# Transposes of a second row tile set between the first V matmuls, with its layernorm root moved up and a quarter of the first tile normed on ScalarE

## The chip, the cores and the metric

One core of one Trainium2 chip. The time is the device time of one execution in microseconds (us); the span in a profile is from the core's first to its last instruction. Every run named here is of the state fast.

## The reference, cut to what matters

A transformer layer of one sequence: 2048 rows, width 1024, 32 heads of 32, a window of 256, then a feed-forward part of width 3584.

```python
x = A_x
h  = x + attention(layernorm(x) @ wqkv) @ wo       # causal, window 256
h2 = h + silu(layernorm(h) @ w1) @ w2
# layernorm(x) = (x - mean) / sqrt(var + 1e-5), over 1024 columns
```

The first matmul on x comes only after the first 128 rows of x are loaded, normed and transposed (7.93 us after the start in the profile before). That head of the kernel is what the change touches.

## The kernel before: the parts concerned

```python
    load_x(0, 0)                   # row tile 0 of x, 128 x 1024 bf16
    load_wqkv(2 * D)               # V weights, columns 0 to 511: 1 MB
    load_x(0, 1, nc.scalar)
    load_x(0, 2)
    load_wqkv(2 * D + 512)         # V weights, columns 512 to 1023
    load_x(0, 3)
    load_wqkv(0)
    # ... identity; 11 matmuls on zeros: 0.43 us apart up to 5.35 us, then 0.21

    def ln_first(xt, st, rs, j, half_done=None, ahead=None):
        ln_stats(xt, st, j, half_done)              # VectorE: 2 x bn_stats, bn_aggr
        nc.scalar.activation(out=rs[:, j:j + 1], in_=st[:, j, 1:2], func=ACT.Sqrt, bias=eps[:], scale=1.0)
        if ahead is not None:
            ln_half(ahead[0], ahead[1], 0)          # first half of the next tile's statistics
        nc.vector.reciprocal(out=rs[:, j:j + 1], in_=rs[:, j:j + 1])
        for h in range(4):
            ln_norm(xt[:, h * 256:(h + 1) * 256], st, rs, j)     # VectorE

    def turn_first(xt, dst, j):
        for h in range(4):
            for i in range(2):                      # two 128x128 transposes on TensorE into PSUM
                kt = h * 2 + i
                nc.tensor.transpose(out=tp_ps[h][:, i * P:(i + 1) * P], in_=xt[:, kt * P:(kt + 1) * P], identity=ident[:])
            nc.scalar.copy(out=dst[:, h * 2:(h + 1) * 2, j * P:(j + 1) * P],
                           in_=tp_ps[h][:, 0:256].rearrange("p (k q) -> p k q", q=P))

    # v_group(b, j, c, copy, between): 8 matmuls, row tile j times half c of the V weights,
    # then one PSUM copy; between(kt) runs ahead of matmul kt
    ln_first(x_ring[0], st, rs, 0, None, (x_ring[1], half))
    turn_first(x_ring[0], lnT_b[0], 0)
    ln_first(x_ring[1], st, rs, 1, half)

    def turn_1(kt):
        if kt == 7:
            turn_first(x_ring[1], lnT_b[0], 1)

    v_group(0, 0, 0, act, turn_1)
    ln_first(x_ring[2], st, rs, 2)
    v_group(0, 1, 0, act)
    ln_first(x_ring[3], st, rs, 3)
    ln_transpose(x_ring[3], lnT_b[0], 3)            # tile 3 is transposed by a DMA
    # ... three more weight loads
    v_group(0, 0, 1, act)
    turn_first(x_ring[2], lnT_b[0], 2)
    v_group(0, 1, 1, act)
    # ... (0,2,0), (0,2,1), (0,3,0), (0,3,1), then the Q and K groups and all the rest
```

The V groups' matmuls are numbered in their order on TensorE: 1 to 8 is (tile 0, half 0), 9 to 16 (tile 1, half 0), 17 to 24 (tile 0, half 1), the 25th begins (tile 1, half 1).

The softmax here doesn't subtract the row's maximum and nothing guards it: scores larger than these inputs give would overflow.

## Time and profile before

| | before |
|---|---|
| time, median of 3 (later of 6) | 693.14 (693.18) us |
| span of the profiled run | 691.8 us |
| TensorE busy | 99% of the span |
| first x tile landed | 4.42 us |
| first V weight block landed | 7.74 us |
| first transpose, first V matmul, 25th V matmul | 7.04, 7.93, 14.56 us |

The two landings are those of the last part of each transfer on its semaphore. The views that carry the rest are shown in the prediction.

### The profile page before, as it was taken

To read this page: it belongs to the slowest core of one execution; us is meant where nothing else is said; L and a number is where in the kernel's file an instruction comes from. 1 tells how busy PE (TensorE), PEld (TensorE's weight loads), DVE (VectorE), ACT (ScalarE), POOL (GpSimd) and SP (SyncE) were. 2 spreads that over 40 slices of the span, in tenths; PEclk is the share of its full clock that TensorE was granted. 3 is DMA by queue.
4 is the path that set the end of the run, shared out by engine and by line. 5 is a ranking of instruction groups with operands and counts; after the bars stand their busy time and mean duration, and the time that the engine had idled before them with its cause. 6 is when DMAs were issued, how large, how long until landed. Compare 5 with 4: busy or idle time off the path is not lost.

```text
span 691.8 us, 14227 instructions
## 1 busy us (share of the span) xinstructions
PE 686.3 (99%) x6011; PEld 331.3 (48%) x6011; DVE 291.6 (42%) x616; ACT 240.9 (35%) x460; POOL 160.4 (23%) x295
## 2 busy tenths in 40 slices
PE   8999999999999999999999999999999999999998
PEld 3444555555555555544444444444444444444445
DVE  6267646744444439533315133343133251333111
ACT  4316666666766676521310033300133100233000
POOL 1006666656666665500000000000000000000000
PEclk9999999999999999999999999999999999999999
DMA  7732132126241899971023310022300033100010
GB/s 243 259 50 83 36 77 67 26 58 189 72 131 17 240 237 275 213 282 48 14 77 115 91 39 0 1 91 70 84 0 1 9 103 94 39 1 1 30 39 24
DMA packets 76464, 60.96 MB, mean 88 GB/s; under 512 B 50288, under 2 KB 60528, under 8 KB 76400
## 3 DMA queue, kind: packets, MB, share of 16 engines
q1 hardware_dynamic: 76256, 59.78, 31.0%
q8 instruction: 47, 0.77, 0.5%
q10 hardware_dynamic: 144, 0.26, 0.1%
q14 instruction: 17, 0.14, 0.1%
HBM read 39.85 MB, written 8.39 MB: 70 GB/s over the span
## 4 chain that ended last, share of the span: by engine, by line
PE 99%; DMA 1%; DVE 0%; issue 0%
PE hacc L597 19%; PE hacc L634 17%; PE acc L245 17%; PE acc L634 10%; PE acc L597 9%; PE acc L235 8%; PE acc L266 7%; PE o_ps L378 5%; PE sc L298 3%; PE hacc L266 1%; PE sc L350 1%; PE sc L324 1%; DMA r_o<-in_A_x_dram 1%; PE tp L213 0%; DVE ln_st L166 0%; DVE r_o L194 0%
## 5 line engine op out<-in xcount | busy, mean ns | idle before, releaser
L368 POOL TENSOR_SCALAR_AFFINE_SELECT r_e<-r_e 128x512 bf16<-128x512 bf16 (+1 forms) x288 | 157.4, 561 | 127.0 <-ACT r_e L358 63.1
L634 PEld LDWEIGHTS <-r_a 128*128 128x128 bf16 x952 | 90.9, 98 | 103.0
L597 PEld LDWEIGHTS <-r_w 128*128 128x128 bf16 x896 | 87.4, 98 | 105.1
L634 PE MATMUL hacc<-r_a 128*128 128x512 bf16 (+2 forms) x616 | 122.5, 360 | 0.0
L597 PE MATMUL hacc<-r_e,r_w 128*128 128x512 bf16 x456 | 100.9, 379 | 0.0
L310 ACT ACTIVATE r_e<-sc 128x768 bf16<-128x768 f32 x96 | 78.2, 814 | 48.3 <-PE sc L298 46.1
L606 ACT ACTIVATE r_n<-hacc 128x512 f32<-128x512 f32 x30 | 17.9, 597 | 178.9 <-PE hacc L597 178.9
L634 PE MATMUL acc<-r_a 128*128 128x512 bf16 x336 | 74.0, 379 | 0.0
L245 PEld LDWEIGHTS <-r_w 128*128 128x128 bf16 x512 | 44.2, 97 | 46.1 <-issue 1.0
L245 PE MATMUL acc<-r_t,r_w 128*128 128x512 bf16 x256 | 63.4, 379 | 0.0
L247 DVE CAST r_a<-acc 128x512 bf16<-128x512 f32 x56 | 38.6, 690 | 55.8 <-PE acc L245 55.6
L245 PE MATMUL acc<-r_w 128*128 128x512 bf16 x256 | 59.9, 379 | 0.0
L378 PEld LDWEIGHTS <-r_e 128*128 128x128 bf16 x1440 | 47.4, 96 | 17.9
L266 PE MATMUL acc<-r_o,r_a 128*128 128x512 bf16 x208 | 51.9, 379 | 0.0
L597 PE MATMUL acc<-r_e,r_w 128*128 128x512 bf16 x216 | 49.1, 379 | 0.0
L378 PE MATMUL o_ps<-r_a,r_e 128*128 128x33 bf16 x1440 | 48.1, 178 | 0.0
L311 ACT ACTIVATE r_e<-sc 128x256 bf16<-128x256 f32 x96 | 37.6, 392 | 0.0
L649 DVE SCALAR_TENSOR_TENSOR r_t<-hacc,r_t 128x512 bf16<-128x512 f32 (+2 forms) x22 | 14.0, 635 | 55.6 <-PE hacc L634 55.6
L649 DVE SCALAR_TENSOR_TENSOR r_t<-acc,r_t 128x512 bf16<-128x512 f32 x12 | 8.3, 692 | 64.2 <-PE acc L634 64.2
L607 DVE SCALAR_TENSOR_TENSOR r_a<-r_n,hacc 128x512 bf16<-128x512 f32 x30 | 20.6, 688 | 33.0 <-ACT r_n L606 33.0
L597 PE MATMUL hacc<-r_a,r_w 128*128 128x512 bf16 x144 | 32.9, 379 | 0.0
L266 PEld LDWEIGHTS <-r_a 128*128 128x128 bf16 x256 | 21.8, 97 | 22.3
(75 smaller groups left out, 534.2 us busy)
## 6 DMA issues: line engine op xcount, KB each, us to landing
r_w<-in_B_w_dram SPq DMA_DIRECT2D x8, 896.0 KB, 5.1
r_a<-in_B_w_dram SPq DMA_DIRECT2D x7, 1024.0 KB, 7.6
r_w<-in_A_wqkv_dram SPq DMA_DIRECT2D x6, 1024.0 KB, 8.8
h_dram<-r_t SPq DMA_DIRECT2D x16, 256.0 KB, 2.9
r_t<-h_dram SPq DMA_DIRECT2D x16, 256.0 KB, 2.8
out_dram<-r_t SPq DMA_DIRECT2D x31, 128.0 KB, 1.7
r_o<-in_A_x_dram SPq DMA_DIRECT2D x15, 256.0 KB, 3.9
r_e<-h_dram SPq DMA_DIRECT2D x3, 1024.0 KB, 5.6
```

The source lines that it names most:

```text
L235: nc.tensor.matmul(acc, lhsT=lnT_b[b % 2][:, kt, j * P:(j + 1) * P], rhs=wv[:, kt, c * 512:(c + 1) * 512], start=(kt == 0), stop=(kt == KT ...
L245: nc.tensor.matmul(acc, lhsT=wqk[:, kt, col0:col0 + P], rhs=lnT_b[b % 2][:, kt, :], start=(kt == 0), stop=(kt == KT - 1))
L247: copy(out=(qT, kT)[which][b][:, g, :], in_=acc)
L266: nc.tensor.matmul(acc, lhsT=qT[b][:, g, j * P:(j + 1) * P], rhs=wo[:, g, c * 512:(c + 1) * 512], start=(g == 0), stop=(g == G - 1))
L298: nc.tensor.matmul(sc[hh // 2][half * 64:half * 64 + 64, hh % 2, col:col + qb - qa], lhsT=kT[t // 4][r0:r0 + DH, g, k0:k0 + 64], rhs=qT[b] ...
L310: nc.scalar.activation(out=tri[:, :, :, 64:256], in_=both, func=ACT.Exp, scale=scale)
L311: nc.scalar.activation(out=e[:, 1024:1280].rearrange("p (h q) -> p h q", q=P), in_=bank[:, :, 192:320], func=ACT.Exp, scale=scale)
L368: nc.gpsimd.affine_select(out=dst, in_=src, pattern=[[0, n] for n in dst.shape[1:-1]] + [[sgn, P]], compare_op=ALU.is_ge if upper else ALU ...
L378: nc.tensor.matmul(o_ps[pair][:, qt * 2 + hh, 0:VW], lhsT=chunk_of(i, bank, piece, pair, hh), rhs=v[:, b * 4 + kt, g * 4 + pair * 2 + hh, ...
L597: nc.tensor.matmul(acc, lhsT=w1[:, kt, ft * P:(ft + 1) * P], rhs=ln2T[b][:, kt, :], start=(kt == 0), stop=(kt == KT - 1))
L634: nc.tensor.matmul(acc[:, 0:c1 - c0], lhsT=gT[:, ft, j * P:(j + 1) * P], rhs=w2[ft // 4][:, ft % 4, c0:c1], start=(ft == 0), stop=(ft == F ...
L649: nc.vector.scalar_tensor_tensor(out=t_out[j % 2][:, c0:c1], in0=acc[:, 0:c1 - c0], scalar=0.5, in1=t_in[j % 2][:, c0:c1], op0=ALU.mult, o ...
```

## The change

Its intent: take the holes out of TensorE's first seven microseconds. (a) The last quarter of tile 0 is normed on ScalarE as x times 1/sigma plus a shift, so that VectorE reaches tile 1's statistics one instruction sooner. (b) Tile 1's root (the square root of its variance, on ScalarE) goes between tile 0's copies on ScalarE. (c) Tile 1's four pairs of transposes are spread over the end of its predecessor group and the beginning of its own, and the predecessor's PSUM copy is held back behind them. (d) Tiles 2 and 3 are normed in one instruction each.

```diff
 ...
+    def ln_first(xt, st, rs, j, parts, on_act=0):
+        if on_act:
+            shift = small.tile([P, 2], F32, name="ln_shift", tag="ln_shift")
+            nc.scalar.activation(out=shift[:, 0:1], in_=st[:, j, 0:1], func=ACT.Identity, scale=-1.0)
         nc.vector.reciprocal(out=rs[:, j:j + 1], in_=rs[:, j:j + 1])
+        if on_act:
+            nc.scalar.activation(out=shift[:, 1:2], in_=shift[:, 0:1], func=ACT.Identity, scale=rs[:, j:j + 1])
+        n = 1024 // parts
+        for h in range(parts):
+            part = xt[:, h * n:(h + 1) * n]
+            if h < parts - on_act:
+                ln_norm(part, st, rs, j)
+            else:
+                nc.scalar.activation(out=part, in_=part, func=ACT.Identity, bias=shift[:, 1:2], scale=rs[:, j:j + 1])
 ...
-    ln_first(x_ring[0], st, rs, 0, None, (x_ring[1], half))
-    turn_first(x_ring[0], lnT_b[0], 0)
-    ln_first(x_ring[1], st, rs, 1, half)
+    ln_stats(x_ring[0], st, 0)
+    ln_root(st, rs, 0)
+    ln_half(x_ring[1], half, 0)
+    ln_first(x_ring[0], st, rs, 0, 4, 1)
+    ln_stats(x_ring[1], st, 1, half)
+    for h in range(4):
+        turn_first(0, h)
+        if h == 2:
+            ln_root(st, rs, 1)
+    ln_first(x_ring[1], st, rs, 1, 4)
+    ln_stats(x_ring[2], st, 2)
+    held = []
     def turn_1(kt):
         if kt == 7:
-            turn_first(x_ring[1], lnT_b[0], 1)
-    v_group(0, 0, 0, act, turn_1)
-    ln_first(x_ring[2], st, rs, 2)
-    v_group(0, 1, 0, act)
-    ln_first(x_ring[3], st, rs, 3)
+            turn_first(1, 0)
+    def turn_1_rest(kt):
+        if kt == 2:
+            turn_first(1, 3)
+            act(**held.pop())
+            ln_root(st, rs, 2)
+    v_group(0, 0, 0, lambda **args: held.append(args), turn_1)
+    turn_first(1, 1)
+    turn_first(1, 2)
+    v_group(0, 1, 0, act, turn_1_rest)
+    ln_first(x_ring[2], st, rs, 2, 1)
+    ln_stats(x_ring[3], st, 3)
+    ln_root(st, rs, 3)
+    ln_first(x_ring[3], st, rs, 3, 1)
 ...
```

More of the change, by code (lines that the diff above doesn't have):

```diff
@@ L198, in ln_transpose, with ln_root, turn_first @@
         nc.sync.dma_start_transpose(out=dst[:, :, j * P:(j + 1) * P], in_=xt)
-    def ln_first(xt, st, rs, j, half_done=None, ahead=None):
-        ln_stats(xt, st, j, half_done)
+    def ln_root(st, rs, j):
         nc.scalar.activation(out=rs[:, j:j + 1], in_=st[:, j, 1:2], func=ACT.Sqrt, bias=eps[:], scale=1.0)
-        if ahead is not None:
-            ln_half(ahead[0], ahead[1], 0)
+    def ln_first(xt, st, rs, j, parts, on_act=0):
+        if on_act:
+            shift = small.tile([P, 2], F32, name="ln_shift", tag="ln_shift")
+            nc.scalar.activation(out=shift[:, 0:1], in_=st[:, j, 0:1], func=ACT.Identity, scale=-1.0)
         nc.vector.reciprocal(out=rs[:, j:j + 1], in_=rs[:, j:j + 1])
-        for h in range(4):
-            ln_norm(xt[:, h * 256:(h + 1) * 256], st, rs, j)
-    def turn_first(xt, dst, j):
-        for h in range(4):
-            for i in range(2):
-                kt = h * 2 + i
-                nc.tensor.transpose(out=tp_ps[h][:, i * P:(i + 1) * P], in_=xt[:, kt * P:(kt + 1) * P], identity=ident[:])
-            nc.scalar.copy(out=dst[:, h * 2:(h + 1) * 2, j * P:(j + 1) * P],
-                           in_=tp_ps[h][:, 0:256].rearrange("p (k q) -> p k q", q=P))
+        if on_act:
[7 more added lines that the diff above has]
+                nc.scalar.activation(out=part, in_=part, func=ACT.Identity, bias=shift[:, 1:2], scale=rs[:, j:j + 1])
+    def turn_first(j, h):
+        for i in range(2):
+            kt = h * 2 + i
+            nc.tensor.transpose(out=tp_ps[h][:, i * P:(i + 1) * P], in_=x_ring[j][:, kt * P:(kt + 1) * P], identity=ident[:])
+        nc.scalar.copy(out=lnT_b[0][:, h * 2:(h + 1) * 2, j * P:(j + 1) * P],
+                       in_=tp_ps[h][:, 0:256].rearrange("p (k q) -> p k q", q=P))
     def ln_tiles(tag):
@@ L462 @@
     v_group(0, 0, 1, act)
-    turn_first(x_ring[2], lnT_b[0], 2)
+    for h in range(4):
+        turn_first(2, h)
     v_group(0, 1, 1, act)
```

## The prediction

The durations that stand between the marks (dummy, root, copy) are those of the kernel before. The forecast's sum was 0.05 + 0.12 + 0.45 - 0.20, about 0.42 from the rounded terms and given as about 0.41 us (14.56 - 14.15). Of its terms only the 0.05, the first V matmul at 7.88 instead of 7.93, rested on what is cut, and its working is gone; copy 3's start at 8.57 in part 2 rested on the same estimate and costs nothing in the sum.

> **What bounds the kernel now.** I read the page's busy shares first, then the chain of work that ended last, cut to its first 25 us, then the timelines of TensorE, VectorE and ScalarE in the same stretch, then the groups by shape for durations.
>
> ```profile
> PE 686.3 (99%) x6011; PEld 331.3 (48%) x6011; DVE 291.6 (42%) x616; ACT 240.9 (35%) x460; POOL 160.4 (23%) x295
> ...
> PE 99%; DMA 1%; DVE 0%; issue 0%
> ```
>
> TensorE is the bound, and the chain leaves it only in the head: nothing but TensorE work after the first transposes. A change in the first V groups can therefore only shift when the dense stretch starts; whatever it saves there should arrive at the end of the run unchanged. The chain's beginning (start, length, what):
>
> ```profile
> 0.80 3.62 DMA r_o<-in_A_x_dram
> 4.45 1.30 DVE ln_st L166 x2
> ...
> 6.63 0.36 DVE r_o L194
> ...
> 7.04 1.05 PE tp L213 x8
> 8.09 1.51 PE acc L235 x7
> 9.60 1.01 PE tp L213 x8
> 10.61 3.67 PE acc L235 x17
> 14.28 0.45 PE tp L213 x8
> 14.73 8.63 PE acc L235 x40
> ```
>
> The reader is to see that eight transposes take 0.45 us when their data is there (at 14.28), but about 1.0 us at 7.04 and at 9.60, where they are paced by the normalization that feeds them. The last line runs at 8.63/40 = 0.216 us a matmul.
>
> The budget: the first transpose starts at 7.04, the 25th matmul at 14.56 (start in the timeline). In between stand 24 matmuls x 0.216 = 5.18 and 24 transposes x 0.056 (0.45/8) = 1.34, together 6.52 us, in 7.53 us of time. So 1.01 us is lost, in three places: 0.45 in tile 0's transposes (7.04 to 7.93 instead of 0.45 long), 0.12 waiting between matmul 7 of group (tile 0, half 0) and tile 1's first transpose (9.44 to 9.56), 0.45 in tile 1's transposes (9.56 to 10.45). That is the most this change can win: 0.15% of 693.
>
> What paces the two sets, on VectorE and ScalarE:
>
> ```profile
> 6.63 1.11 DVE L194 TENSOR_SCALAR r_o<-r_o,st_a,rs_a 128x256 bf16<-128x256 bf16 x4
> 7.66 0.69 DVE L166 BATCH_NORM_STATS2 ln_st<-r_o 128x6 f32<-128x512 bf16 x1
> 8.38 0.21 DVE L174 BATCH_NORM_AGGREGATE st_a<-ln_st 128x2 f32<-128x12 f32 x1
> 8.95 0.16 DVE L205 RECIPROCAL rs_a<-rs_a 128x1 f32<-128x1 f32 x1 [0.36 <-ACT rs_a L202]
> 9.15 1.11 DVE L194 TENSOR_SCALAR r_o<-r_o,st_a,rs_a 128x256 bf16<-128x256 bf16 x4
> ```
>
> ```profile
> 7.36 1.20 ACT L214 COPY r_w<-tp 128x256 bf16<-128x256 bf16 x4 [1.05 <-PE tp L213]
> 8.63 0.29 ACT L202 ACTIVATE rs_a<-st_a,eps 128x1 f32<-128x1 f32 x1
> ```
>
> One norm of a quarter is 0.34 long and they start every 0.257; the copies start every 0.263. Tile 1's second half of statistics waits for tile 0's four norms, and all of tile 1's chain follows from it.
>
> [...]the 128x1 dummy, 202 to 203 ns; the root with a pointer bias, 294; the 128x256 copy, mean 387 [...]
>
> ```profile
> L194 DVE TENSOR_SCALAR r_e<-r_e,st_b,rs_b x12: 535/539/543, 378.1 to 575.1; 128x1024 bf16<-128x1024 bf16 x12
> ```
>
> 768 more elements cost 0.20 us, so one norm of a whole tile (0.54) replaces four quarters (1.11). [...]
>
> **The change part by part.** The count of matmuls, transposes, copies and bytes is unchanged; ScalarE gets three instructions. I carried the changed order forward with these durations and the handoffs seen before: 0.035 us from a VectorE end to a ScalarE start and back, 0.06 from a VectorE or ScalarE end to the matmul that waits for it, copies from PSUM 0.036 after the end of the transpose's record (which is 0.219 long), a norm 0.20 after its reciprocal starts.
>
> Part 1, a quarter of tile 0 on ScalarE. Sign change of the mean beside the reciprocal (done by 6.42), its product with the reciprocal 6.63 to 6.92[...]. Three quarters remain on VectorE, the third done at 7.49 as before. So the last two transposes start at 7.67 instead of 7.80, and the transposes are over 0.13 earlier. But the norm stands ahead of the copies on the same engine[...]. Win 0.05, not 0.13; the weights land at 7.74 and would allow little more.
>
> Part 2, tile 1's statistics. With one VectorE norm less ahead of them, the second half starts 0.257 earlier (7.41), the aggregate is over at 8.34. The root now stands between copies 2 and 3 instead of after copy 3: copy 2 starts at 7.98, root 8.37 to 8.66. Copy 3 is pushed to 8.57 to 8.98, and matmul 6, its first user, is due at 9.17, so that costs nothing. Reciprocal 8.70, norms of tile 1 from 8.90: their ends are 9.24, 9.50, 9.75, 10.01 instead of 9.50, 9.76, 10.01, 10.27.
>
> Part 3, transposes among matmuls. Matmul 6 ends its slot at 9.39, so tile 1's first pair starts at once (data 9.30), then matmul 7 (9.50), the second pair at 9.72 (data 9.56), the third at 9.83 (data 9.81), over at 9.94. Then matmul 0 of (tile 1, half 0) wants copy 0 of tile 1: pair at 9.45 + 0.219 + 0.036 = 9.70, copy to 10.07, matmul at 10.14: a gap of 0.20. Matmuls 0 and 1, the fourth pair at 10.57, matmuls 2 to 7 end their slots at 11.98. The held PSUM copy of (0, half 0), put behind the four transposed copies, runs 11.15 to 11.78; the next group into that bank needs it at 11.98 and its weights at 11.16. Margin 0.14. Eight matmuls to 13.71, eight transposes of tile 2 to 14.15. The matmul that started at 14.56 starts at 14.15.
>
> Sum: of the lost 1.01, 0.40 stays in tile 0's transposes and first copy and 0.20 before (1, half 0). Saved 0.05 + 0.12 + 0.45 - 0.20 = about 0.41 us.
>
> Part 4, tiles 2 and 3 in one norm each: 0.57 less on VectorE per tile, so tile 3 is normed by about 15.2 instead of 16.50, and its DMA transpose (issue to landing 2.8 us) lands near 18.1 instead of 19.35, while its group would want it at 19.74 - 0.41 = 19.33. Without this part, 19.35 would just have become a wait. It earns nothing itself. Later weight loads start earlier as well, hidden.
>
> Result: 693.14 - 0.41 = 692.73, rounded 692.7.
>
> **The rivals.** First, the gain is eaten by a new wait in ScalarE's order. The norm, root and held copy share the engine with eight copies. If the ScalarE norm is 0.2 longer than estimated, the first matmul slips to 8.08 and the gain falls to 0.2 to 0.3 (693.0); if the held copy is 0.3 late, the bank wait at 11.98 takes 0.15 (692.9). For it: margins of 0.14 us. [...]
>
> Second, the gain is larger: the transposes leave no holes because the copy gap of 0.20 is partly closed, or tile 0's copies are not delayed by the norm. At the limit all 0.57 of tile 1's loss and 0.13 of tile 0's come back: 0.70, 692.4.
>
> Third, the head's gain is lost later: the dense part waits for something with a fixed time, a weight load or a tile's transpose. Against: loads for the Q and K groups land by 14.46 and 27.44, groups that use them come at 22.9 and 29.8; after the head TensorE waits for no engine or transfer in the list of waits. This would give 693.1.
>
> Fourth, slower: the start of the chain is a DMA and the executions differ by 0.5 us (692.88 to 693.38), more than the effect. The reading could land above before without cause.
>
> **Range and chances.** The modelled gain is 0.2 to 0.6; medians of three runs scatter by some 0.25 each. Together 692.1 to 693.3, middle 692.7. Two per cent would be 14 us, fourteen times the whole loss in the head: faster 0.005, same 0.99, slower 0.005.
>
> **What would show it.** Right: the first transposes stay at 7.04, first V matmul near 7.88, aggregate of tile 1 ending near 8.34, tile 1's norms from 8.90, the 25th matmul near 14.15, first Q group near 22.95 instead of 23.36, the rest shifted alike; [...]whole-tile norms 0.54. Wrong: a 25th matmul at 14.4 or later, ScalarE's norm ending past 7.7, a wait before the third V group, or a Q group early and an end that is not.

## The result, and the profile after

The changed kernel took 693.03 us (median of 6, 692.88 to 693.41), the kernel before 693.18 (median of 6). The ratio, which is the mean time of one kernel's fast runs over that of the other's of the same rounds and so not quite the ratio of these medians, is 0.9999 with an interval of 0.9986 to 1.0012: the same, and inside the predicted range. That range (692.1 to 693.3) also holds the time of the kernel before, so the time alone says nothing of the mechanism. A second measurement (r1 below), beside other runs of the kernel before, gave 693.33 against 693.33.

The beginning of the chain of work that ended last, changed kernel (start, length, what):

```profile
1.26 6.61 DMA r_w<-in_A_wqkv_dram
...
7.92 1.67 PE acc L245 x7
9.59 0.11 PE tp L223 x2
9.70 0.22 PE acc L245
9.92 0.22 PE tp L223 x4
10.14 0.03 issue
10.16 0.61 PE acc L245 x2
10.77 0.11 PE tp L223 x2
10.88 2.59 PE acc L245 x12
...
13.90 0.45 PE tp L223 x8
14.35 8.63 PE acc L245 x40
```

Two things are to be seen. The one long row of eight slow transposes (9.60, 1.01 us) is gone: tile 1's four pairs take 0.11 us each, between matmuls. And the chain no longer begins with the x tile and its norm: it begins with the load of the first V weight block, which lands at 7.88 and holds the first V matmul until 7.92, though the transposes were through at 7.61. The timelines of ScalarE and VectorE in the changed kernel answer to those shown of before:

```profile
6.83 0.60 ACT L217 ACTIVATE r_o<-r_o,ln_shift,rs_a 128x256 bf16<-128x256 bf16 x1
7.34 0.90 ACT L224 COPY r_w<-tp 128x256 bf16<-128x256 bf16 x3
8.18 0.29 ACT L201 ACTIVATE rs_a<-st_a,eps 128x1 f32<-128x1 f32 x1
8.38 0.35 ACT L224 COPY r_w<-tp 128x256 bf16<-128x256 bf16 x1
```

```profile
6.44 0.86 DVE L194 TENSOR_SCALAR r_o<-r_o,st_a,rs_a 128x256 bf16<-128x256 bf16 x3
7.21 0.69 DVE L166 BATCH_NORM_STATS2 ln_st<-r_o 128x6 f32<-128x512 bf16 x1
7.93 0.21 DVE L174 BATCH_NORM_AGGREGATE st_a<-ln_st 128x2 f32<-128x12 f32 x1
...
8.70 1.12 DVE L194 TENSOR_SCALAR r_o<-r_o,st_a,rs_a 128x256 bf16<-128x256 bf16 x4
```

The order is as designed: three quarters on VectorE, one on ScalarE for 0.60 us, the root between copies.

**A clock that can be compared.** The first x tile landed between 3.82 and 4.42 us after the first instruction in the profiles, whatever the kernel, and everything up to the first transpose follows it rigidly: the first transpose's weights are loaded 2.60 to 2.61 us after that landing in every profile but the one that delays it on purpose. So the tables count from the landing of the first x tile. (The change moves the x buffer as well, as the experiments will show, but no effect on this landing is seen: it came 3.04 to 3.62 us after its issue in the four profiles with unmoved buffers, 3.02 to 3.59 in the ten with moved ones.) Without that, 0.19 us of the 0.38 that lie between the two 25th matmuls (14.56 and 14.19) would be put down to the change, though it is only x that came earlier. The 25th V matmul is given by the load of its weights, since the trace of the changed kernel lacks 116 matmul records but no weight load.

| us after the first x tile's landing | before | changed | changed, second profile |
|---|---|---|---|
| first V weight block landed | 3.31 | 3.65 | 3.67 |
| first V matmul | 3.50 | 3.69 | 3.71 |
| tile 1's aggregate done | 4.17 | 3.91 | 3.91 |
| 25th V matmul, weights loaded | 10.09 | 9.91 | 9.93 |
| last weight load of the kernel | 684.26 | 684.08 | 684.10 |

The gain in the head is 0.18 us in the first profile and 0.16 in the second, 0.17 in the mean, and it reaches the end undiminished: from the 25th V matmul to the last weight load are 674.18 us before and 674.17 after. The prediction had 0.41. The first V matmul came 0.19 later than before, not 0.05 earlier, because the weight block took 0.34 us longer to land. Nothing in the diff touches that load. Why it slowed down is the question that the experiments had to settle.

### The profile page after: what moved, and what is told of

It is laid out like the page before. It is cut to its first block, busy times and chain, and to the rows that moved or that the text cites. A ratio compares the mean times of both kernels' runs of the same rounds, so it can differ in the third digit from the quotient of the medians.

```text
span 691.4 us, 14107 instructions
## 1 busy us (share of the span) xinstructions
PE 677.0 (98%) x5895; PEld 331.6 (48%) x6011; DVE 290.5 (42%) x609; ACT 241.8 (35%) x463; POOL 160.4 (23%) x295
## 4 chain that ended last, share of the span: by engine, by line
PE 97%; issue 1%; DMA 1%; SPq 0%; DVE 0%
PE hacc L628 19%; PE hacc L665 17%; PE acc L255 16%; PE acc L665 10%; PE acc L628 9%; PE acc L245 8%; PE acc L276 7%; PE o_ps L388 5%; PE sc L308 3%; PE hacc L276 1%; DMA r_w<-in_A_wqkv_dram 1%; PE sc L360 1%; PE sc L334 1%; PE tp L223 0%; SPq L135 0%
## 5 line engine op out<-in xcount | busy, mean ns | idle before, releaser
L255 PE MATMUL acc<-r_t,r_w 128*128 128x512 bf16 x233 | 60.3, 379 | 2.4 <-issue 1.7
L255 PE MATMUL acc<-r_w 128*128 128x512 bf16 x240 | 58.0, 379 | 1.5 <-issue 0.9
L276 PE MATMUL acc<-r_o,r_a 128*128 128x512 bf16 x188 | 49.5, 379 | 1.9 <-issue 1.3
```

The source lines that it names most:

```text
L255: nc.tensor.matmul(acc, lhsT=wqk[:, kt, col0:col0 + P], rhs=lnT_b[b % 2][:, kt, :], start=(kt == 0), stop=(kt == KT - 1))
L276: nc.tensor.matmul(acc, lhsT=qT[b][:, g, j * P:(j + 1) * P], rhs=wo[:, g, c * 512:(c + 1) * 512], start=(g == 0), stop=(g == G - 1))
```

## The experiments

Twelve runs were made, each timed in five rounds against the kernel before; all gave correct results. Times are medians, with the kernel before of the same rounds in brackets; no interval excludes 1 but that of the delayed kernel. The readings are from each run's one profile. All counts are from the landing of the first x tile.

| run | weight block | first V matmul | 25th V weights | time (before) |
|---|---|---|---|---|
| e1 quarter on VectorE | 3.31 | 3.50 | 9.85 | 693.21 (693.41) |
| e2 turns together | 3.63 | 3.67 | 9.83 | 693.07 (693.41) |
| e3 weights halved | 2.12 (half) | 3.51 | 9.76 | 693.11 (693.41) |
| e4 statistics delayed | 3.66 | 4.85 | 13.42 | 695.41 (693.41) |
| r1 changed again | 3.67 | 3.71 | 9.93 | 693.33 (693.33) |
| e5 pair before 6 | 3.68 | 3.72 | 9.74 | 693.12 (693.33) |
| e6 halved and 6 | 2.15 (half) | 3.52 | 9.67 | 693.09 (693.33) |
| e7 all halved and 6 | 2.16 (half) | 3.51 | 9.61 | 693.17 (693.33) |
| e8 before, shifted | 3.69 | 3.73 | 10.09 | 693.08 (693.24) |
| e9 changed, aligned | 3.26 | 3.52 | 9.75 | 692.96 (693.24) |
| e10 aligned and 6 | 3.35 | 3.51 | 9.61 | 692.71 (693.24) |
| e11 tiles in quarters | 3.63 | 3.67 | 9.88 | 693.22 (693.24) |

### e1: the quarter back on VectorE

```diff
-    ln_first(x_ring[0], st, rs, 0, 4, 1)
+    ln_first(x_ring[0], st, rs, 0, 4)
```

> The changed kernel with tile 0 normed wholly on VectorE again, all else as changed. Theory A (the first weight block holds the first V matmul, so the ScalarE quarter has nothing left to win there): the last pair of transposes of tile 0 starts some 0.1 to 0.15 us later than in the changed kernel, the first V matmul still follows the landing of the weight block by about 0.05 us, tile 1's statistics end 0.26 us later, tile 1's first transposes still find their data within 0.1 us of their turn, and the 25th V matmul and the end move by less than 0.1 us. Theory B (the quarter earns its keep, as the prediction had it by way of tile 1's statistics): the 25th V matmul and the end come 0.2 to 0.3 us later than in the changed kernel.

The first V matmul came at 3.50, and the 25th at 9.85, 0.06 earlier than in the changed kernel, not later. Theory A expected about no difference and theory B a loss of 0.2 to 0.3, so B fell; but A was not right either, for the weight block landed at 3.31, as in the kernel before, and held nothing.

### e2: tile 1's transposes in one row

```diff
     def turn_1(kt):
         if kt == 7:
-            turn_first(1, 0)
+            for h in range(4):
+                turn_first(1, h)
-    v_group(0, 0, 0, lambda **args: held.append(args), turn_1)
-    turn_first(1, 1)
-    turn_first(1, 2)
-    v_group(0, 1, 0, act, turn_1_rest)
+    v_group(0, 0, 0, act, turn_1)
+    ln_root(st, rs, 2)
+    v_group(0, 1, 0, act)
```

> The changed kernel with tile 1's eight transposes in one row before the last matmul of the first group again, and the PSUM copy of that group at once. Theory A (early statistics alone remove the stall; the interleaving only moves it): transposes of tile 1 start about 9.4, the set takes 0.5 to 0.6 us instead of 0.89 in the kernel before, the second group's first matmul follows at about 10.2, and its end and the 25th V matmul come within 0.1 us of the changed kernel, perhaps earlier. Theory B (the interleaving hides the wait for the norms): 0.2 to 0.4 us later than the changed kernel.

The eight transposes took 0.59 us in one row (chain of this run):

```profile
7.77 1.67 PE acc L245 x7
9.44 0.59 PE tp L223 x8
10.03 3.67 PE acc L245 x17
```

The 25th matmul's weights came at 9.83, 0.08 before the changed kernel: theory A. Where the weight block is late, the changed kernel without its interleaving removes as much of the stall, and spreading the transposes out adds a small hole (the 0.03 "issue" at 10.14 in the changed kernel is its visible rest; the first matmul of the second group waits for a copy). That is shown for this late weight block only; no run tries it with an early one. This profile then lost 0.43 us at about 286 us, in a wait that other runs show too (see the rivals, below).

### e3: the first weight block in two transfers

```diff
-    load_wqkv(2 * D)
+    for k in (0, 4):
+        nc.sync.dma_start(out=wv[:, k:k + 4, 0:512], in_=wqkv_v[:, k:k + 4, 2 * D:2 * D + 512])
```

> The changed kernel with the first weight block loaded as two transfers of four row tiles each. Theory A (the weight block held the first V matmul at 7.92, 0.3 us after the transposes were through): the first half lands by about 6.5, the first V matmul starts some 0.1 us after the first ScalarE copy ends (about 7.75), and the whole head and the end come 0.15 to 0.2 us earlier. Theory B (the first copy on ScalarE, behind the norm quarter, was the hold): first matmul and end within 0.05 us of the changed kernel.

The first V matmul moved from 3.69 to 3.51 and the 25th from 9.91 to 9.76: theory A, for the head. (The end moved by 0.07 only, since this profile lost 0.07 at 286 us.) The weight block was the hold in the changed kernel. With it out of the way the first V matmul stands where it stood in the kernel before: the ScalarE quarter wins nothing there.

### e4: tile 0's chain delayed

```diff
+    spare = small.tile([P, 2, 6], F32, name="spare", tag="spare")
+    for _ in range(2):
+        ln_half(x_ring[0], spare, 0)
     ln_stats(x_ring[0], st, 0)
```

> The changed kernel with two useless statistics instructions (0.61 us each in sequence) ahead of tile 0's chain. Both theories say that a delay of the head arrives whole at the end. Theory A (0.3 us of slack against the weight block): the transposes start 1.22 us later, the first V matmul 0.9 us later, the 25th V matmul and the end about 0.9 to 1.0 us later. Theory B (no slack): 1.2 us later at the end. If the dense part absorbed delays (third theory), the end would move by less than the 25th V matmul.

The profile missed both numbers, for TensorE's granted clock fell: it was 0.50 from 8.3 to 14 us, after TensorE had stood idle for 2.95 us between the matmuls on zeros and the first transposes. (Before, that idle time was 1.09 us and the clock from 5 to 13 us was 1.00; that the longer idle time brought the fall is not shown.) The stretches 5 to 8.3, 8.3 to 14 and 14 to 20 us of this run (length, then busy time and instructions of five engines, clock, DMA):

```profile
5.00:8.30 3.30, 0.39 (x2) 0.00 (x0) 3.19 (x9) 0.68 (x3) 0.00 (x0) 0.89 1.08 368
8.30:14.00 5.70, 5.67 (x24) 2.78 (x25) 3.98 (x12) 2.92 (x9) 0.00 (x0) 0.50 1.06 344
14.00:20.00 6.00, 6.00 (x35) 3.03 (x34) 2.82 (x7) 3.71 (x11) 0.00 (x0) 0.96 0.03 11
```

At clock 0.50 each matmul took 0.427 us instead of 0.216. Four of the five executions have a mean clock of 0.995 to 0.998 and took 695.23 to 696.80 us; one kept 1.000 and took 693.94. Against the changed kernel's 692.88 to 693.46 in eleven runs that last one is 0.5 to 1.1 longer, which fits the 0.9 of theory A, but one run does not prove the slack. What the run does show is that the delay arrives whole: from the 25th matmul to the end are 674.17 us here too.

### r1, e5, e6, e7: the changed kernel again, an earlier pair, loads in halves

```diff
 # e5: tile 1's first pair before matmul 6 instead of 7
-        if kt == 7:
+        if kt == 6:
             turn_first(1, 0)
 # e6: e5 and e3 together.  e7: e6, and the second weight block in halves too:
-    load_wqkv(2 * D + 512)
+    for k in (0, 4):
+        nc.sync.dma_start(out=wv[:, k:k + 4, 512:1024], in_=wqkv_v[:, k:k + 4, 2 * D + 512:3 * D])
```

> The changed kernel once more, for the scatter between executions. Counted from the landing of the first x tile: if the weight block lands 3.65 us later, the first V matmul is at 3.69 and the 25th at 9.96, as in its first profile; if it lands by 3.35 (theory A of the earlier runs: the load rate differs between executions), the first V matmul is at 3.50 to 3.53 and the 25th at 9.80 to 9.83. From first to 25th V matmul 6.27 to 6.31 in either case, against 6.64 in the kernel before.

> The changed kernel with tile 1's first pair of transposes before matmul 6 instead of 7 of the first group. Theory A (the hole of 0.19 us before the second group is the latency from the first pair through its copy): first to 25th V matmul 6.10 to 6.17 instead of 6.27; where the weight block is early, the pair may wait up to 0.1 for its data. Theory B (another wait takes its place: the held copy's bank or the second weight block): stays at 6.25 or more.

> Both: first weight block in halves and the pair before matmul 6. Counted from the landing of the first x tile: first V matmul at 3.50 to 3.53, second group's first at 5.65 to 5.70. At the slow load rate the second weight block (landing at 7.6) holds the third group, so the 25th V matmul stays at 9.78 to 9.83; at the fast rate it comes at 9.66 to 9.70.

> As the run with both, and the second weight block in halves too, so that the third group can begin on the first of them. 25th V matmul at 9.66 to 9.72 after the landing of the first x tile at either load rate, 0.4 to 0.45 us earlier than in the kernel before (10.14) and 0.1 to 0.3 earlier than the changed one; time 692.7 to 692.9.

The changed kernel repeated itself within 0.02 us, weight block at 3.67 again. The earlier pair (e5) gives 9.74 against 9.92: the hole ahead of the second group, which the prediction had put at 0.20, is closed. With the first block in halves 9.67; with both 9.61, the earliest of all. r1, e5 and e7 went as expected in the head (e5 0.03 better: 6.07 us from the first to the 25th matmul). e6 did not: at its slow load rate the 25th matmul was expected to stay at 9.78 to 9.83, held by a second weight block that lands at 7.6; the block landed at 7.35 and the matmul itself came at 9.72. The time of e7, 693.17, missed the 692.7 to 692.9 that were expected. The times stay within the scatter.

By now a pattern stood out that chance did not explain: the unsplit weight block landed 3.31 us after x in the kernel before and in e1, and 3.63 to 3.68 in the changed kernel (twice), e2, e4 and e5. The two fast ones are those without the `ln_shift` tile. That tile sits in the pool of small tiles ahead of the large buffers. In the built programs the weight buffer starts at byte 17408 of each partition in the kernel before and in e1, a multiple of 1024 (and so of 256, as the expectation under e8 names it), but at 17472 in the changed kernel, 64 bytes further, and at 17600, 192 bytes further, in e4. The next two runs test the start address alone (e8 adds one small memset on GpSimd with it, e9 nothing).

### e8: the kernel before, shifted by 64 bytes

```diff
     nc.gpsimd.memset(v[:, :, :, DH:VW], 1.0)
+    pad = const.tile([P, 16], F32, name="pad")
+    nc.gpsimd.memset(pad[:], 0.0)
```

> The kernel before with 64 unused bytes a partition ahead of its large buffers, as the changed kernel has by its new two-column tile. In the runs so far the first weight block landed 3.32 us after the first x tile in the two kernels whose buffers start at a multiple of 256 bytes (before, and the quarter on VectorE), and 3.63 to 3.68 in all five unsplit ones that start 64 or 192 bytes past one. Theory A (the start address sets the load rate): 3.63 to 3.68 here, second weight block near 7.35 instead of 6.73, the first V matmul near 3.69 instead of 3.51, tile 1's DMA-loaded data in time, the 25th V matmul's weights at 10.10 to 10.20. Theory B (ScalarE's instructions, or chance): 3.32 and nothing moves.

Weight block at 3.69, second block at 7.35, first V matmul at 3.73: theory A, but for a few hundredths. The stretch 5 to 13 us of four kernels, in one fence each (last column GB/s, before it the DMA engines' share): before, before shifted, changed, and changed and aligned (e9).

```profile
5.00:13.00 8.00, 6.91 (x39) 2.89 (x38) 7.07 (x23) 4.18 (x13) 0.00 (x0) 1.00 1.08 388
```

```profile
5.00:13.00 8.00, 7.56 (x40) 3.16 (x39) 7.07 (x23) 4.37 (x13) 0.00 (x0) 1.00 1.09 357
```

```profile
5.00:13.00 8.00, 7.41 (x41) 3.28 (x40) 6.68 (x20) 5.20 (x16) 0.00 (x0) 1.00 1.09 359
```

```profile
5.00:13.00 8.00, 7.82 (x42) 3.57 (x42) 6.83 (x21) 5.19 (x16) 0.00 (x0) 1.00 1.08 387
```

The DMA engines are equally busy (share 1.08 and 1.09) and move 8% less when the buffers start 64 bytes off. All fourteen profiles divide so: 387 to 389 GB/s in the four whose buffers start at a multiple of 1024 bytes, 357 to 360 in the ten that start 64 or 192 bytes past one. (All the large buffers move together, the weights' and the x tiles', so which of them matters is not separated.) The chain of the shifted kernel changes its beginning just as that of the changed kernel did:

```profile
1.26 6.61 DMA r_w<-in_A_wqkv_dram
7.88 0.04 issue
7.92 1.67 PE acc L237 x7
9.59 0.79 PE tp L215 x8
```

The 25th matmul stays at 10.09, as the tile 1 chain was the later one anyway; a later wait for tile 3's transpose adds 0.05. In the old kernel the slower load costs next to nothing; in the changed one it stands on the path.

e4, whose buffers start 192 bytes past a multiple of 1024, moved 360 GB/s, no less than the 357 (e8) and 359 (changed kernel) of those at 64. Why the start address changes the rate is not shown, and the mechanism stays open. That the start address is the cause is shown, by e8 (the block at 3.69 instead of 3.31) and e9 (3.26 instead of 3.65 to 3.67).

### e9: the changed kernel, aligned

```diff
     big = ctx.enter_context(tc.tile_pool(name="big", bufs=1))
+    tail = ctx.enter_context(tc.tile_pool(name="tail", bufs=1))
 ...
-            shift = small.tile([P, 2], F32, name="ln_shift", tag="ln_shift")
+            shift = tail.tile([P, 2], F32, name="ln_shift", tag="ln_shift")
```

> The changed kernel with its new two-column tile put behind the large buffers, so that they start where they did before. Theory A: first weight block 3.32 after the first x tile, first V matmul at 3.51 to 3.53 instead of 3.69, 25th V matmul's weights at 9.76 to 9.82 instead of 9.92, tile 3's transpose lands 2.8 us after its issue instead of 3.2. Theory B: 3.65 and all as in the changed kernel.

Weight block at 3.26, first V matmul at 3.52, 25th at 9.75: theory A, with 0.01 more than it asked. The chain begins with the x tile again, and not with the weights:

```profile
0.81 3.16 DMA r_o<-in_A_x_dram
...
6.58 1.08 PE tp L224 x8
7.66 1.51 PE acc L246 x7
```

The program differs from the changed kernel in the place of an eight-byte tile alone, and so in the start of the large buffers. Against the kernel before the head now gains 0.34 us; the side effect had cost 0.16 of it. Against e1, which has the same aligned buffers and no ScalarE quarter (9.85), the quarter earns 0.10.

### e10: aligned, and the pair before matmul 6

```diff
 # e9 and e5 together
```

> The same with tile 1's first pair of transposes before matmul 6: the candidate for the best version, without split loads. 25th V matmul's weights 9.60 to 9.66 after the landing of the first x tile, against 10.09 before, 9.92 changed, 9.61 with all loads halved. Time 692.7 to 692.9.

9.61 in the head, equal to the version with all loads in halves and without their extra transfers: 0.48 us earlier than the kernel before. Its five executions took 692.62 to 693.03 (median 692.71), the nine of before in the same rounds 692.92 to 693.46 (median 693.24). It is the fastest version by median, but the ratio of 0.9993 has an interval of 0.9981 to 1.0006, so the time by itself does not prove it. Nor does all of the head's gain arrive in this profile: 0.19 is lost at about 286 us (see the rivals, below), and the last weight load comes 0.29 earlier after x than before, 683.98 against 684.26.

### e11: tiles 2 and 3 in quarters again

```diff
-    ln_first(x_ring[2], st, rs, 2, 1)
+    ln_first(x_ring[2], st, rs, 2, 4)
 ...
-    ln_first(x_ring[3], st, rs, 3, 1)
+    ln_first(x_ring[3], st, rs, 3, 4)
```

> The changed kernel with tiles 2 and 3 normed in four quarters each again. Theory A (the whole-tile norms keep tile 3's DMA transpose ahead of its group): VectorE is done with tile 3 1.15 us later, the transpose lands near 19.7 instead of 18.5, its group would start at 19.3, so TensorE waits 0.3 to 0.4 us there and the Q groups and the end come as much later. Theory B (slack): nothing moves after the 25th V matmul.

Theory A. The chain of this run goes through tile 3's norm and its DMA transpose:

```profile
14.97 1.13 DVE r_o L194 x4
16.10 0.02 issue
16.11 3.22 DMA r_w<-r_o
19.34 0.04 issue
19.38 3.63 PE acc L245 x16
```

The 25th matmul is at 9.88, within 0.03 of the changed kernel, but the first Q group is 0.35 later (18.73 against 18.38). So the part of the change that looks like tidying up guards 0.35 us here, twice what the changed kernel gains. But here the transpose goes into a shifted buffer and takes 3.22 us; with aligned buffers it would take 2.81 and be issued some 0.15 earlier, as in e9, and land about 14.9 after x, when e9's group starts at about 15.0. That is an estimate from e9 and e11: with aligned buffers the quarters would cost little or nothing. No run shows it.

## Why the prediction was right or wrong

- **The class and the time: right.** 0.15% was the most that the holes could give, and the time stayed within scatter. A kernel with no gain at all would have fitted the range too, so only the steps inside test the reasoning.
- **First transposes where they were: right.** 2.61 us after x in both kernels.
- **Part 1, the first V matmul 0.05 earlier: wrong.** It came 0.19 later after x. Two errors. "The weights land at 7.74 and would allow little more" took the load of an unchanged transfer as given; the new tile had moved its destination, and the block landed 0.34 later after x. And with that put right (e9) the matmul is at 3.52, not at the 3.46 that the prediction's 7.88 means: 0.06 late. The shift's product started 0.10 us after the reciprocal's end instead of 0.035, with a semaphore instruction of its own ahead of it, and the norm took 0.60 us, somewhat more than the estimate; the first copy, queued behind, passes that on. What the ScalarE quarter earns, 0.10 in e9 against e1, lies after the first V matmul (3.52 against 3.50), by way of tile 1's statistics (3.91 against 4.16).
- **Part 2, tile 1's statistics: right.** The aggregate was to be done at 8.34, which is 3.92 after x; it was done at 3.91. The root between the copies cost nothing.
- **Part 3, from the first to the 25th V matmul: right.** Predicted 14.15 - 7.88 = 6.27 us; measured 14.19 - 7.92 = 6.27, against 6.64 before, and 6.28 in e9, where the weights are in time, so the late weights are not what made it fit. The hole ahead of the second group was predicted at 0.20 and is 0.19 (9.98 to 10.16); e5 closed it. What the prediction did not see is that the interleaving itself need not be what wins: with a late weight block one row of transposes does as well (e2).
- **Part 4, whole-tile norms: needed in this kernel (e11), but not for the reason given.** The prediction had a wait of 0.02 without them (19.35 against 19.33); e11 has 0.35, by the estimate under e11 all of it from the moved buffers. The landing came 0.6 later after x than estimated: the transpose was issued 0.2 later, and into the shifted buffer it took 3.21 us from issue to landing (2.81 in e9, 2.83 before) instead of 2.8.
- **The sum, 0.41: mis-sized.** Measured 0.17 from x to the 25th matmul. The missing 0.24 is 0.16 for the slower load (e9 against the changed kernel) and, near enough, 0.06 for the first matmul behind the ScalarE norm; the rest, 0.02, is no more than the two profiles of the changed kernel differ by.
- **The rivals.** A new wait in ScalarE's order came only as those 0.06 us. The second, a larger gain, did not come: the hole stayed at 0.19. The fourth, that scatter between executions hides the effect, is so for the times. The third, a gain lost later, did not come in the changed kernel, but the reason given against it was too strong: from the first Q group to the last weight load are 665.70 us in ten of the fourteen profiles, but 0.07 to 0.43 more in the other four (e2, e3, e5, e10). There TensorE waits at about 286 us for the last DMA transpose of the feed-forward's first block (in e2 it lands at 286.51 and the next weights are loaded at 286.68). Each of these kernels has one profile, so whether the wait comes with the kernel or with the execution is not known, and why it comes was not followed up.

## What to carry to other kernels

A new tile of a few bytes can move every buffer behind it (here by 64 bytes, with 357 to 359 GB/s instead of 387 to 389 from 5 to 13 us, e8 and the changed kernel against before, e1, e9 and e10): after a change, compare the start addresses of the large DMA targets as one compares the diff, and put small tiles behind the large buffers, which e9 shows to work (weight block at 3.26). The runs tried starts at a multiple of 1024 bytes and 64 and 192 past one, so which alignment is enough is not shown. Count from an event that the change can't touch, or that is seen not to move with it, such as the landing of the first input here, when differences are smaller than the scatter of the start. When several chains end within 0.2 us of each other, undoing any one part of a change shows little, and only a run that takes the latest of them away shows what holds.
